# The attention output projection (Wo) as seven half-size products in two waves of eight token tiles, with the weight sums formed during attention

## The chip, the cores and the metric

The kernel runs on one core of one Trainium2 chip. The metric is device time in microseconds (us) for one execution, the median of several. The profile is one further execution, recorded by the hardware profiler.

## What is computed

An adaLN-conditioned block on 2048 tokens of width 1024. Part A is attention with a small recurrent memory (32 heads of 128, segments of 32 tokens, 8 memory rows); part B is a token-shift mixer and an MLP. Cut to what matters here:

```python
h = _layernorm(x) * (1 + ca) + sa
# A: per head q, k, v = h @ Wq, Wk, Wv; o = softmax(q k^T * scale, masked) @ v
o = jnp.einsum('bhte,hed->btd', o, Wo)      # the product that changes: [2048, 4096] @ [4096, 1024]
x = x + ga * o
h = _layernorm(x) * (1 + cb) + sb
x = x + gb * B(h, w1, w2, w3, w4)           # B starts with layernorm(h) @ w1
```

The kernel estimates the memory rows from segment means instead of running the recurrence, checks the estimate (`check_a`, `check_b` in the code), and holds a second, sequential path, which a flag selects at run time and which does not run on this input.

## The kernel before

**Attention.** A loop over 16 pairs of heads interleaves, unit by unit, the projections of the next pair (`P_units`, with `D_units` as seven half-size products in fp16, the Winograd form of Strassen's scheme) with the attention of the current heads (`scores`, `outs`). The context of a head is turned by a DMA transpose (`flip`), and `keep_o` (L755) stores it with a POOL DMA as `OTx_d`, by blocks of 512 tokens and groups of 8 heads. `guard_units` (L674, L678) loads w3 and w4 in 28 pieces into a one-buffer pool (`wstream`) and sums squares on ACT. About 1.75 heads of attention are left as a tail, which is interleaved with the first Wo units. `preload` fetches the first Wo and context tiles ahead.

**Wo.** `W_units(blk)` handles 512 tokens in four blocks. For each column half `n2` (512 columns) it runs over four groups of 8 heads (`hc`) and four token tiles (`tt`), 8 matmuls each into one PSUM bank per tile (L901), so 1024 matmuls of 128x128 by 128x512 in all. At the last group DVE multiplies the bank by the row `ga_b` into the fp32 row tile `x1` (L906). Wo is streamed in 1 MiB pieces (L884, four buffers), contexts in 1 MiB pieces (L867, six buffers); `paced` and `pace` tie the first loads to matmuls so that SP issues them in a chosen order.

**Rows.** `C1a(t)` takes a 128-token tile through: load x (L1018, SP), add (L1019, POOL), store `x_d` (ACT queue), first layernorm (`ln_act`: bn_stats on DVE L104, power on POOL L110, scale and shift on ACT L1009), modulation (L1024, L1025, DVE), store `u_d`, second layernorm. `C1b(t)` turns the tile by DMA into `zT` (L1037, ACT queue). `lagged` and `interleave` place four tiles beside the Wo units of the next block; the last four go beside `A_units(0)` and `A_units(1)`, the product with w1 (L1068) with GELU on ACT (L1069). `A_units(3)` needs the last tile. `check_b` (L984 to L999) reduces the tests to one flag; its instructions are issued early in Wo.

**What sets the order.** Each engine runs its instructions in order, and SP, ACT and POOL each issue their DMAs in order with the rest of their queue. A scheduler puts the instructions of the program into per-engine orders by dependence and place in the program; buffers of a pool are reused in turn, and a tile waits until the former user of its buffer is done. `keep_order` marks instructions whose order is fixed.

Of the kernel before, what the change touches and what calls it, by code (L numbers as in the profile page):

```python
# [9 lines left out]
BF16 = mybir.dt.bfloat16  # L10
# [13 lines left out]
H = 32  # L24
# [36 lines left out]
def kernel(ctx, tc, A_x, A_mem0, A_Wq, A_Wk, A_Wv, A_Wo, A_seg_len, B_x, B_w1, B_w2, B_w3, B_w4, c, w_mod, out,  # L61
# [14 lines left out]
    OTx_d = dram.tile([4, 4, DH, 8, 512], BF16, name="OTx_d")  # L76
    Mnew_d = dram.tile([P, KT, NSEG * M], F32, name="Mnew_d")
# [23 lines left out]
    def layernorm_stats(pool, src):  # L101
        st = pool.tile([P, 2, 6], F32, name="ln_st")
        for i in range(2):
            nc.vector.bn_stats(out=st[:, i, :], in_=src[:, i * 512:(i + 1) * 512])  # L104
        mv = pool.tile([P, 2], F32, name="ln_mv")
        nc.vector.bn_aggr(out=mv[:], in_=st[:])
        ve = pool.tile([P, 1], F32, name="ln_ve")
        nc.vector.tensor_scalar(ve[:], mv[:, 1:2], EPS, None, ALU.add)
        rstd = pool.tile([P, 1], F32, name="ln_rstd")
        nc.gpsimd.tensor_tensor(rstd[:], ve[:], mhalf[:], ALU.pow)  # L110
        return mv[:, 0:1], rstd[:]
# [55 lines left out]
    def first_pass(late_hook):  # L167
# [14 lines left out]
        wsq = mpool.tile([P, 28], F32, name="wsq")  # L182
        rin_all = mpool.tile([P, H, NT], F32, name="rin_all")
# [466 lines left out]
        pre = {}  # L650

        def preload():

            pre["ot"] = [prep.tile([P, 4, 512], BF16, name=f"pre_o{i}") for i in range(2)]
            pre["wo"] = [prep.tile([P, 4, 512], BF16, name=f"pre_w{i}") for i in range(2)]
            for i in range(2):
                nc.sync.dma_start(pre["wo"][i][:], Wo2[i * 512:(i + 1) * 512, 0:512].rearrange("(h p) n -> p h n", p=P))
                nc.sync.dma_start(pre["ot"][i][:], OTx_d[0, 0, :, 4 * i:4 * i + 4])
# [6 lines left out]
        def guard_units():  # L665

# [12 lines left out]
            nop = lambda: None  # L679
            for i in range(28):  # L680
                units += [load(i), nop, nop, square(i)]
            return units
# [69 lines left out]
        def keep_o(h):  # L752
            OT = last_ot[h] = state.pop(("ot", h))
            flat = OT[:].rearrange("p t c -> p (t c)")[:, 64:64 + S]
            nc.gpsimd.dma_start(OTx_d[:, h // 8, :, h % 8, :].rearrange("b d t -> d b t"), flat.rearrange("p (b t) -> p b t", t=512))  # L755
# [83 lines left out]
        RG = ExitStack()  # L839
        rgp = RG.enter_context(tc.tile_pool(name="x_gb", bufs=1, side="right"))  # L840
        RX = ExitStack()
        rp = RX.enter_context(tc.tile_pool(name="x_rows", bufs=1, side="right"))
        gb_b = rgp.tile([P, D], F32, name="gb_b")
# [3 lines left out]
        RW = ((ga_b, rows_d[0]), (sb_b, rows16_d[0]), (cb1_b, rows16_d[1]))  # L847
        acc_pools[:] = [psA, psA, psX, psX2]
        acc_ctr[0] = 3
        RO = ExitStack()  # L850
        wspR = RO.enter_context(tc.tile_pool(name="x1_wsR", bufs=4, side="right"))
        otcp = RO.enter_context(tc.tile_pool(name="x1_ot", bufs=1, side="right"))
        ws_pools[:] = [wspR]
        ots = {}

        paced = {}

        def pace(ld, mm):
            if mm is not None:
                tc.add_manual_dep(ld.ins, mm.ins.name, mybir.DependencyInfo(mybir.DependencyClass.Sync, mybir.DependencyReason.DATA), reason="order of loads")  # L860

        def load_ot(j, mm=None):
            if j >= 16:
                return
            ot = otcp.tile([P, 8, 512], BF16, name=f"OTc{(j + 2) % 6}")
            n = 6 if j == 3 else 8
            pace(nc.sync.dma_start(ot[:, 0:n], OTx_d[j // 4, j % 4, :, 0:n]), mm)  # L867
            ots[j] = [ot[:, 0:4], ot[:, 4:8]]

        ots[0] = [t[:] for t in pre["ot"]]  # L870

        marks = {}
# [3 lines left out]
        def W_units(blk):  # L876
            st = {}

            def load_w(n2, hc, mm=None):
                if (blk, n2, hc) == (0, 0, 0):  # L880
                    st[n2, hc] = [t[:] for t in pre["wo"]]
                elif (n2, hc) not in st:
                    woc = ws_tile([P, 8, 512])
                    pace(nc.sync.dma_start(woc[:], Wo2[hc * 1024:(hc + 1) * 1024, n2 * 512:(n2 + 1) * 512].rearrange("(h p) n -> p h n", p=P)), mm)  # L884
                    st[n2, hc] = [woc[:, 0:4], woc[:, 4:8]]

            def mk(n2, hc, tt):
                def f():
                    cs = slice(n2 * 512, (n2 + 1) * 512)
                    if (hc, tt) == (0, 0):  # L890
                        st[n2] = [acc_tile() for _ in range(4)]
                    if (n2, hc, tt) == (0, 3, 0):
                        for i in range(4):
                            x1s[blk * 4 + i] = xpools["tp4"].tile([P, D], F32, name="x1")
                    accs = st[n2]
                    if tt == 0:
                        load_w(n2, hc)
                    ot, woc = ots[blk * 4 + hc], st[n2, hc]
                    for hl in range(8):
                        h = hc * 8 + hl  # L900
                        mm = nc.tensor.matmul(accs[tt][:], lhsT=ot[hl // 4][:, hl % 4, tt * P:(tt + 1) * P], rhs=woc[hl // 4][:, hl % 4, :], start=(h == 0), stop=(h == H - 1))  # L901
                    if blk == 0 and tt == 0:
                        for f in paced.pop((n2, hc), ()):
                            f(mm)
                    if hc == 3:
                        marks[blk] = nc.vector.tensor_tensor(x1s[blk * 4 + tt][:, cs], accs[tt][:], ga_b[:, cs], ALU.mult)  # L906
                    if n2 == 1 and tt == 3:
                        load_ot(blk * 4 + hc + 6)
                return f
            return [[[mk(n2, hc, tt) for tt in range(4)] for hc in range(4)] for n2 in range(2)], load_w  # L910

        W0, W0_load = W_units(0)
        W0_load(0, 1)
        load_ot(1)
        paced[0, 0] = [lambda mm: W0_load(0, 2, mm), lambda mm: load_ot(2, mm)]
        paced[0, 1] = [lambda mm: W0_load(1, 0, mm)]
        paced[0, 2] = [lambda mm: W0_load(1, 1, mm), lambda mm: [pace(nc.gpsimd.dma_start(t[:], src.partition_broadcast(P)), mm) for t, src in RW]]
        paced[1, 0] = [lambda mm: W0_load(1, 2, mm), lambda mm: load_ot(3, mm)]
        paced[1, 1] = [lambda mm: W0_load(0, 3, mm)]
        paced[1, 2] = [lambda mm: W0_load(1, 3, mm), lambda mm: load_ot(4, mm)]  # L920
        paced[0, 3] = [lambda mm: load_ot(5, mm)]
        load_wo2(NHP - 2)
        interleave(att[done:], M_units(NHP - 3) + [lambda: load_wo2(NHP - 1)] + W0[0][0] + W0[0][1])
        for u in W0[0][2]:
            u()
# [3 lines left out]
        for u in M_units(NHP - 2):  # L929
            u()  # L930
# [3 lines left out]

# [1147 lines left out]
```

## Time and profile before

| what | value |
|---|---|
| median of 3 runs | 1466.67 us (1463.84 to 1469.35) |
| the profiled execution's own time | 1465.43 us |
| its span | 1463.6 us |
| mean granted TensorE clock | 0.994 |
| tail of attention and hand-over to Wo | 757 to 797 us |
| Wo after that | 797 to 993 us |
| product with w1 | 993 to 1048 us |
| MLP and the rest | 1048 to 1464 us |

In a group line of the profile the fields are: line, engine, operation, tiles written and read, shapes, count; then the busy time of the group in us and the mean duration of one in ns; then the idle time of the engine just before them and what ended most of it. Matmuls are pipelined, so durations overlap. In a line by stretches (windows) each stretch has its length, the busy time and count of PE, weight loads, DVE, ACT and POOL, the granted clock, the DMA share and GB/s. In the timeline, a line has start, duration, engine, line and operation, with idle time before it in brackets.

### The profile page before, as it was taken

To read this page: it belongs to the slowest core of one execution; us is meant where nothing else is said; L and a number is where in the kernel's file an instruction comes from. 1 tells how busy PE (TensorE), PEld (TensorE's weight loads), DVE (VectorE), ACT (ScalarE), POOL (GpSimd) and SP (SyncE) were. 2 spreads that over 40 slices of the span, in tenths; PEclk is the share of its full clock that TensorE was granted. 3 is DMA by queue.
4 is the path that set the end of the run, shared out by engine and by line. 5 is a ranking of instruction groups with operands and counts; after the bars stand their busy time and mean duration, and the time that the engine had idled before them with its cause. 6 is when DMAs were issued, how large, how long until landed. Compare 5 with 4: busy or idle time off the path is not lost.

```text
span 1463.6 us, 24731 instructions
## 1 busy us (share of the span) xinstructions
PE 1421.2 (97%) x9254; PEld 752.2 (51%) x9254; DVE 897.9 (61%) x1945; ACT 683.3 (47%) x1439; POOL 347.5 (24%) x494
## 2 busy tenths in 40 slices
PE   6999999999999999999998999999998999999998
PEld 4665555565555555555563444444443444444443
DVE  6627767677777777676651436335254578666684
ACT  3636666666566566566650122114466650056400
POOL 6020010000000000000001323203023664645625
PEclk9999999999999999999999999999998999999999
DMA  9778777796777787667599999965499774477812
GB/s 336 279 225 195 170 165 168 172 214 140 179 167 168 176 195 176 161 154 168 118 240 311 365 311 368 320 167 164 141 282 239 232 255 141 150 227 253 282 41 79
DMA packets 404149, 303.48 MB, mean 207 GB/s; under 512 B 199082, under 2 KB 356778, under 8 KB 402226
## 3 DMA queue, kind: packets, MB, share of 16 engines
q1 hardware_dynamic: 365904, 242.06, 62.0%
q10 hardware_dynamic: 29330, 30.89, 6.9%
q0 software_dynamic: 8784, 28.85, 6.3%
q8 instruction: 74, 1.21, 0.4%
q14 instruction: 57, 0.47, 0.1%
HBM read 200.56 MB, written 50.63 MB: 172 GB/s over the span
## 4 chain that ended last, share of the span: by engine, by line
PE 80%; DMA 10%; issue 3%; DVE 3%; ACT 3%; POOL 1%; SPq 0%; ACTq 0%; DVEq 0%; POOLq 0%
PE acc L619 31%; PE acc L901 7%; PE bank_b L1291 7%; PE bank_b L1240 6%; PE acc L1068 4%; PE acc L328 4%; PE bank_d L1240 3%; PE acc L318 3%; PE bank_d L1291 2%; PE bank_e L1291 2%; PE ps_o L730 2%; PE ps_s L713 2%; PE acc L1168 2%; PE bank_e L1240 1%; DMA xt<-in_A_x_dram 1%
## 5 line engine op out<-in xcount | busy, mean ns | idle before, releaser
L901 PE MATMUL acc<-wstream,OTc 128*128 128x512 bf16 x960 | 209.2, 379 | 4.2 <-DMA OTc<-OTx_d 3.6
L619 PEld LDWEIGHTS <-T 128*128 128x128 f16 x1408 | 130.8, 97 | 120.3 <-issue 1.4
L587 ACT COPY snap<-acc 128x480 f32<-128x480 f32 x264 | 146.7, 564 | 87.5 <-PE acc L619 82.5
L619 PE MATMUL acc<-hh,T 128*128 128x480 bf16 (+1 forms) x704 | 161.9, 366 | 0.3 <-DVE VT L591 0.3
L619 PE MATMUL acc<-hs,T 128*128 128x480 f16 x704 | 157.0, 366 | 0.4 <-ACT snap L587 0.4
L901 PEld LDWEIGHTS <-OTc 128*128 128x128 bf16 x960 | 93.3, 98 | 116.0 <-DMA OTc<-OTx_d 4.3
L1240 PEld LDWEIGHTS <-ring 128*128 128x128 f16 (+1 forms) x784 | 77.3, 99 | 106.4 <-issue 16.3
L755 POOL DMA_DIRECT2D OTx_d<-OT x32 | 24.8, 776 | 445.1 <-DMA OT<-O 366.6
L717 ACT ACTIVATE E<-ps_s 99x495 bf16<-99x495 f32 (+2 forms) x160 | 87.5, 547 | 52.4 <-PE ps_s L713 52.3
L619 PE MATMUL acc<-hh,wq 128*128 128x480 bf16 x464 | 105.1, 366 | 0.0
L737 DVE TENSOR_TENSOR O<-ps_o,rin_all 99x384 bf16<-99x384 f32 (+1 forms) x192 | 97.4, 510 | 3.9
L1205 ACT COPY snap<-bank_b 128x512 f32<-128x512 f32 x72 | 41.9, 587 | 105.3 <-PE bank_b L1291 60.6
L1291 PEld LDWEIGHTS <-hq 128*128 128x128 bf16 (+1 forms) x560 | 54.8, 98 | 66.1 <-DVE hq L1094 0.2
L591 DVE TENSOR_TENSOR KT<-acc,snap 128x480 bf16<-128x480 f32 x116 | 75.1, 655 | 19.8 <-PE acc L619 13.6
L719 DVE TENSOR_TENSOR E<-E,maskB 99x495 bf16<-99x495 bf16 (+1 forms) x128 | 48.2, 377 | 60.8 <-ACT E L717 59.5
L1094 DVE TENSOR_TENSOR ring<-ring 128x1024 f16<-128x1024 bf16 (+1 forms) x64 | 81.2, 1287 | 4.9 <-PE bank_b L1291 4.4
L730 PE MATMUL ps_o<-V,E 99*128 99x129 bf16 (+1 forms) x704 | 80.4, 220 | 3.2 <-DVE E L719 1.6
L1009 ACT ACTIVATE u<-x,ln_nmr,ln_rstd 128x1024 bf16<-128x1024 f32 x16 | 19.7, 1231 | 128.1 <-DMA x_d<-x 76.8
L730 PEld LDWEIGHTS <-E 99*128 99x128 bf16 (+1 forms) x704 | 56.8, 98 | 39.0 <-DVE E L719 3.1
L1244 ACT ACTIVATE hq<-join 128x512 bf16<-128x512 f32 x84 | 52.9, 630 | 43.6 <-DVE join L1248 43.6
L1291 PE MATMUL bank_b<-ring,hq 128*128 128x512 f16 (+1 forms) x336 | 73.2, 379 | 0.0
L591 DVE TENSOR_TENSOR VT<-acc,snap 128x480 bf16<-128x480 f32 x90 | 58.0, 651 | 18.7 <-PE acc L619 14.6
(240 smaller groups left out, 2502.8 us busy)
## 6 DMA issues: line engine op xcount, KB each, us to landing
wstream<-in_A_Wo_dram SPq DMA_DIRECT2D x31, 1024.0 KB, 10.1
OTx_d<-OT POOLq DMA_DIRECT2D x32, 512.0 KB, 7.2
wstream<-in_B_w_dram SPq DMA_DIRECT2D x28, 512.0 KB, 5.8
OTc<-OTx_d SPq DMA_DIRECT2D x14, 1024.0 KB, 7.9
ring<-in_B_w_dram SPq DMA_DIRECT2D x28, 512.0 KB, 6.2
ring<-in_B_w_dram SPq DMA_DIRECT2D x8, 1792.0 KB, 10.9
wq<-in_A_Wq_dram SPq DMA_DIRECT2D x16, 512.0 KB, 4.5
wk<-in_A_Wk_dram SPq DMA_DIRECT2D x16, 512.0 KB, 5.6
```

The costliest lines, as they stand in the source:

```text
L328: nc.tensor.matmul(acc[:, 0:CONV], lhsT=W[:, kt, hl * P:(hl + 1) * P], rhs=hh[:, kt, MAIN:MAIN + CONV], start=(kt == 0), stop=(kt == KT - 1))
L587: nc.scalar.copy(t[:], st[q][bank][:, 0:CH])
L591: nc.vector.tensor_tensor(view(d, i), chunks(st[q][bank]), chunks(st[q][s_]), ALU.add)
L619: nc.tensor.matmul(acc[:, 0:CH], lhsT=B[:, k, :], rhs=A[:, k, :], start=(j in (1, 2, 5) and k == 0), stop=(k == 3), skip_group_check=True)
L717: nc.scalar.activation(E[:rows, 0:o], ps[:rows, 0:o], ACT.Exp, scale=DH ** -0.5)
L730: nc.tensor.matmul(ps[:, i, :], lhsT=state["e", h, t // 5][:k, c:c + P], rhs=V[:k, t, 0:DH + 1], start=True, stop=True)
L737: nc.vector.tensor_tensor(O[:rows, ts[0]:ts[0] + n, :], ps[:rows, 0:n, 0:DH], rin[:, :, None].to_broadcast([rows, n, DH]), ALU.mult)
L901: mm = nc.tensor.matmul(accs[tt][:], lhsT=ot[hl // 4][:, hl % 4, tt * P:(tt + 1) * P], rhs=woc[hl // 4][:, hl % 4, :], start=(h == 0), sto ...
L1068: nc.tensor.matmul(acc[:], lhsT=w1s[:, kt, ct * P:(ct + 1) * P], rhs=zT[:, kt, b * 512:(b + 1) * 512], start=(kt == 0), stop=(kt == KT - 1))
L1094: return nc.vector.tensor_tensor(dst, a, b, op)
L1240: nc.tensor.matmul(acc[:], lhsT=B[:, k, q * P:(q + 1) * P], rhs=A[:, k, :], start=(start and k == 0), stop=(k == 3), skip_group_check=True)
L1291: nc.tensor.matmul(acc[:], lhsT=L3[:, k, i * P:(i + 1) * P], rhs=R3[:, k, :], start=(start and k == 0), stop=(k == 13), skip_group_check=True)
```

## The change

Wo becomes seven products of half size in both tokens, heads and columns (again the Winograd form). Tokens are taken in two waves of 1024; in a wave the halves are two blocks of 512 tokens. Heads are split into even and odd, columns into two halves of 512. So `A11, A12, A21, A22` are contexts of block 0 even, block 0 odd, block 1 even, block 1 odd heads, and `B11 ... B22` quarters of Wo. Each product has K = 2048 (two halves `hf` of 8 head pairs), four token tiles and 512 columns: 64 matmuls. The order is 1, 2, 5, 3, 6, 7, 4; products 1, 2 and 4 use A unchanged, the others fp16 sums, which DVE forms in place (`X_sum`, `sums`, 8 instructions of 128x4096 in a wave).

The weight sums are formed once, in attention: `guard_units` gets 16 more loads of Wo (512 KB), each followed by four DVE subtractions and a POOL store into `WoT_d`. Contexts are stored as `OTw_d`, by parity of the head. Five SBUF slots of 16 KB per partition hold contexts and sums, and later w1, w2, zT's second half and h1T. `tp` has 2 buffers instead of 3. `check_b` comes after `A_units(0)` and `A_units(1)`, and also tests the variances of all 16 tiles (`ves`). `gb_b` is loaded later, `sb_b` and `cb1_b` by `rows2`. Tiles 0 to 3 are chained beside products 7 and 4 of wave 0, tiles 4 to 7 beside products 1, 2, 5 of wave 1, tiles 8 to 11 beside 7 and 4 of wave 1, tiles 12 to 15 beside `A_units(0)` and `A_units(1)`.

```diff
-            nc.gpsimd.dma_start(OTx_d[:, h // 8, :, h % 8, :].rearrange("b d t -> d b t"), ...)
+            nc.gpsimd.dma_start(OTw_d[h % 2][:, :, h // 2, :].rearrange("b d t -> d b t"), ...)
...
+            def wo_load(k):
+                def f():
+                    st["w", k] = ws_tile([P, 2, 2, 512])
+                    keep_order(nc.sync.dma_start(st["w", k][:], Wo2[k * 256:(k + 1) * 256, :].rearrange("(b p) (n c) -> p b n c", p=P, n=2)))
+                return f
+            def wo_sums(k):
+                def f():
+                    t = st["w", k]
+                    B11, B12, B21, B22 = (t[:, b, n, :] for b in range(2) for n in range(2))
+                    keep_order(nc.vector.tensor_tensor(f16(B11), B12, B11, ALU.subtract))
+                    nc.vector.tensor_tensor(f16(B12), B22, B12, ALU.subtract)
+                    nc.vector.tensor_tensor(f16(B22), B22, f16(B11), ALU.subtract)
+                    nc.vector.tensor_tensor(f16(B21), B21, f16(B22), ALU.subtract)
+                    nc.gpsimd.dma_start(WoT_d[:, :, k, :].rearrange("j p c -> p j c"), t[:].rearrange("p b n c -> p (b n) c"))
+                return f
             for i in range(28):
                 units += [load(i), nop, nop, square(i)]
+                if i % 7 in (0, 2, 4, 6):
+                    k = i // 7 * 4 + i % 7 // 2
+                    units += [wo_load(k), nop, nop, wo_sums(k)]
...
+        SLOTS = [{(0, 0): "s0", (0, 1): "s4", (1, 0): "s2", (1, 1): "s1", "X": "s3"},
+                 {(0, 0): "s3", (0, 1): "s4", (1, 0): "s0", (1, 1): "s2", "X": "s1"}]
+        RAW = {1: (0, 0), 2: (1, 0), 3: (1, 1)}
+        SUM = {5: 0, 7: 1, 4: 2, 6: 3}
+        ORDER = (1, 2, 5, 3, 6, 7, 4)
...
+            def fin(t, n, acc, s=None):
+                cs = slice(n * 512, (n + 1) * 512)
+                if s is not None:
+                    nc.vector.tensor_tensor(s[:], acc[:], s[:], ALU.add)
+                nc.vector.tensor_tensor(x1s[t][:, cs], (acc if s is None else s)[:], ga_b[:, cs], ALU.mult)
+            def after(j, i):
+                x, t1, t2 = st[i], 8 * w + i, 8 * w + 4 + i
+                if j == 1:
+                    x["s1"] = snap("stA", x["b"])
+                elif j == 2:
+                    x1_new(t1)
+                    fin(t1, 0, x["d"], x["s1"])
+                elif j == 5:
+                    x["s5"] = snap("stA", x["d"])
+                elif j == 6:
+                    fin(t1, 1, x["d"], snap("st2", x["b"]))
+                elif j == 7:
+                    x1_new(t2)
+                    fin(t2, 1, x["b"], x["s5"])
+                elif j == 4:
+                    fin(t2, 0, x["b"])
+            def unit(j, hf, i):
+                def f():
+                    if i == 0:
+                        b_upto(seq.index((w, j, hf)) + 3)
+                    if hf == 0 and j == 1:
+                        st[i]["b"] = acc_tile()
+                    elif hf == 0 and j in (2, 5):
+                        st[i]["d"] = psB.tile([P, 512], F32, name="acc")
...
+                    for k in range(8):
+                        nc.tensor.matmul(acc[:], lhsT=A[:, k, i * P:(i + 1) * P], rhs=B[:, k, :], start=(j in (1, 2, 5) and hf == 0 and k == 0), stop=(hf == 1 and k == 7), skip_group_check=True)
+                    if hf:
+                        after(j, i)
+                return f
+            def X_sum(hf):
...
+                    nc.vector.tensor_tensor(f16(open_a(w, "X")[:, ks]), Av[w, (1, 0)][:, ks], Av[w, (1, 1)][:, ks], ALU.add)
+            def sums(hf):
...
+                    nc.vector.tensor_tensor(f16(A21), A11, A21, ALU.subtract)
+                    nc.vector.tensor_tensor(f16(A11), f16(X), A11, ALU.subtract)
+                    nc.vector.tensor_tensor(f16(A12), A12, f16(A11), ALU.subtract)
...
-        interleave(att[done:], M_units(NHP - 3) + [lambda: load_wo2(NHP - 1)] + W0[0][0] + W0[0][1])
+        interleave(att[done:], M_units(NHP - 3) + [lambda: load_wo2(NHP - 1)] + U0[1][0:4])
...
+            okx = ck.tile([P, NTT], F32, name="okx")
+            nc.vector.tensor_scalar(okx[:], ves[:], RMAX, None, ALU.is_le)
+            nc.vector.tensor_reduce(oks[:], okx[:], AX.X, ALU.min)
+            nc.vector.tensor_tensor(okm[:], okm[:], oks[:], ALU.mult)
...
+        for u in U0[2][0:4] + [lambda: load_a(0, (0, 0), 0)] + U0[2][4:] + [rows2] + M_units(NHP - 1) + U0[5]:
+            u()
+        interleave(checks, U0[3] + [next_a((0, 0))] + U0[6][0:4] + [next_a((0, 1))] + U0[6][4:])
+        interleave(chain(0), U0[7][0:4] + [next_a((1, 0))] + U0[7][4:] + U0[4][0:4] + [next_a((1, 1))] + U0[4][4:])
...
+        interleave(chain(4), U1[1] + U1[2] + U1[5])
+        for u in U1[3] + [load_w1] + U1[6] + [late_slots]:
+            u()
+        interleave(chain(8), U1[7] + U1[4])
...
+        interleave(chain(12), A_units(0) + A_units(1))
+        check_b()
         for u in A_units(2) + A_units(3):
             u()
```

## The prediction

> **What bounds the kernel now.** I read the page's busy times first, then its chain of work that ended last, then the groups.
>
> ```profile
> span 1463.6 us, 24731 instructions
> ...
> PE 1421.2 (97%) x9254; PEld 752.2 (51%) x9254; DVE 897.9 (61%) x1945; ACT 683.3 (47%) x1439; POOL 347.5 (24%) x494
> ...
> PE 80%; DMA 10%; issue 3%; DVE 3%; ACT 3%; POOL 1%; SPq 0%; ACTq 0%; DVEq 0%; POOLq 0%
> ...
> L901 PE MATMUL acc<-wstream,OTc 128*128 128x512 bf16 x960 | 209.2, 379 | 4.2 <-DMA OTc<-OTx_d 3.6
> ```
>
> TensorE is the bound. The Wo product is L901: 960 matmuls here and 64 more on the preloaded tiles, 1024 in all. The 379 ns is the length of one pipelined matmul, not its price: in steady state 177 of them took 38.37 us (timeline from 954.78), 214 to 217 ns each. I use 214 (the windows of 20 us hold 93 to 94). Next, the busy times by stretch: attention's tail, the hand-over, the rest of Wo, and product w1.
>
> ```profile
> 757.00:778.20 21.20, 19.89 (x179) 11.37 (x176) 10.84 (x36) 8.56 (x21) 2.21 (x6) 1.00 1.05 316
> 778.20:797.00 18.80, 13.83 (x64) 6.15 (x65) 3.29 (x10) 0.00 (x0) 2.61 (x7) 1.00 1.03 293
> 797.00:993.20 196.20, 195.66 (x941) 89.03 (x940) 80.93 (x186) 32.21 (x40) 46.70 (x54) 1.00 0.96 301
> 993.20:1048.40 55.20, 55.20 (x257) 25.05 (x256) 19.50 (x48) 27.76 (x40) 9.93 (x13) 1.00 0.41 128
> ```
>
> The first pair is length and PE busy; the last two columns are DMA share and GB/s. PE stands still for 1.3 + 5.0 + 0.5 = 6.8 us around Wo, nearly all of it waiting for loads. DMA is full (share about 1) at 293 to 316 GB/s from 757 on. DVE has room: 81 of 196 us. In attention (400 to 600 us) PE is busy 199.58 of 200 us, so every stall put there counts.
>
> The last view is the timeline of the row chain (layernorm, modulation, layernorm, per 128-token tile) beside Wo. I looked for whether in-order DVE is on time.
>
> ```profile
> 942.74 2.12 POOL L1019 TENSOR_TENSOR x<-x,xt 128x1024 f32<-128x1024 f32 x1 [0.93 <-issue]
> 943.32 2.10 DVE L1024 TENSOR_TENSOR u<-u,cb_b 128x1024 bf16<-128x1024 bf16 x1 [0.71 <-ACT u L1009]
> ...
> 952.10 0.69 DVE L1024 TENSOR_TENSOR u<-u,cb_b 128x1024 bf16<-128x1024 bf16 x1 [1.49 <-ACT u L1009]
> ...
> 959.47 0.69 DVE L1024 TENSOR_TENSOR u<-u,cb_b 128x1024 bf16<-128x1024 bf16 x1 [1.49 <-ACT u L1009]
> ...
> 969.50 0.67 DVE L906 TENSOR_TENSOR x<-acc,ga_b 128x512 f32<-128x512 f32 x1
> ```
>
> A tile takes 7.4 us (952.10 to 959.47). The bank that L906 empties at 969.50 was full at about 960.6: Wo ends at 993.0, the second column half takes 128 x 0.214 = 27.4 us, and this bank was 5.1 us ahead of the other three. So DVE is already 9 us late, at no cost, since eight banks serve in turn.
>
> **What the Trainium skill says.** "SBUF — State Buffer", section "SBUF: two separate sides": a DVE operation with two SBUF inputs and a GpSimd operation that reads SBUF exclude each other for the whole instruction. The trace agrees: L1024 takes 2.10 us under POOL's addition and 0.69 without. "VectorE: DVE Perf Modes", "The perf-mode tier table": a 16-bit tensor_tensor has a 2x mode, 1224 ns for 2048 elements; the trace has 1222 ns for that shape and 4052 for 7168. For the new 4096-element sums I take 2.4 us between the two rows. "DMA: Bandwidth & Descriptors", "Issuing engines are not separate DMA queues": SP, ACT and POOL transfers share the 16 DMA engines; the full DMA share above agrees.
>
> **The change part by part.** Base: the profiled execution, 1465.4 us; its median over the three runs is 1466.7, 1.2 above, which I add at the end. Orders below are those of the built instructions; L930 to L1108 in this part and the next are lines of the changed kernel where they name L936, L970, L1082 or L1108.
>
> *Fewer matmuls.* 7 products x 64 x 2 waves = 896 instead of 1024: 128 x 0.214 = -27.4 us. fp16 weights load as fast (97 ns, L619). The old stand-stills go, -6.8, and all idle time is now counted anew.
>
> *Attention.* Sixteen times: a load of 512 KB, four subtractions of 512 elements (0.42 us each, L562 to L565, so 27 us of DVE in 630 that is 72% busy), and a 512 KB store from POOL (0.78 us of POOL). T_units already makes 44 such bursts and PE is not idle for them: free. But `wstream` has one buffer, so SP's next load waits for the store, SP's weight loads and transposes queue behind it, and ACT's square waits for the load, with exp and snaps behind that. Turnaround: 0.8 + 7.2 (landing of OTx_d) + 0.3 + 5.8 (landing of wstream) = 14.1 us. The order puts 3 to 5 score groups between the last subtraction and the next square, a group 4.4 us (44.2 us per head pair): 17.6 us mostly, 13.2 twice. I take +2 us; bounds 0 and 24 (15 turnarounds x 1.6 us).
>
> *Tail.* Only 32 Wo matmuls are left to fill attention's latencies instead of 64. The tail shortens by 6.9 us of work; I let 2 us be idle (0 to 4).
>
> *Wave 0, products 1, 2, 5.* The loads up to the first half of A22 (Wo halves, head tiles, wo2) are 10.1 MiB on SP, and 1 MiB of row vectors now goes ahead on POOL: 11.1 MiB = 11.7 MB at 305 GB/s = 38 us from 757, landed about 797; X adds 2.4. PE would come at 757 + 16.3 + 6.9 + 0.9 + 13.7 = 794.8: +4. Then DVE has X's second half, two Macc additions and five sums of 2.4 ahead of the first A12 sum, 16 us against 13.7 of product 5: +2. I take +6 (2 to 12). Later loads of wave 0 (about 20 MiB in 62 us up to wave 1's second half product, 340 GB/s) are tight, and hidden by the 4-deep ring in my reckoning; uncovered they cost up to 8.
>
> *Wave 1, product 2 to 5.* Product 5 reuses the four psB banks of product 2, so it waits for DVE's first addition there. DVE's order puts ahead of it, from product 6 of wave 0 on: 21 evacuations x 0.68 = 14.3; six tiles' first half (1.9 each) 11.2; five tiles' second half (3.2 each) 16.2; seven sums x 2.4 = 16.8. That is 58.5 us in the 59.8 us that PE needs there (280 matmuls), before any gap. The chain of four tiles lasted 39 us before (933.5 to 972.6) for some 23 us of DVE work; half of those gaps get filled, and POOL's additions lock DVE. Left: 10 us of gaps. I take +9 (4 to 13), and +1.5 (0 to 3) for product 3, whose last bank waits for an ACT snap behind two row steps.
>
> *End of Wo.* `check_b` moves behind A_units(0, 1) and gets the variances of all tiles. PE's order has its L1082 matmul before A_units(2), 256/2 x 0.214 = 27.4 us after Wo's end E. Before, the last tile's variance was done at 1021.0, E + 28. Now its chain starts late: tiles 8 to 11 begin 30.4 us before E and need 33.4 (933.5 to 966.9) plus about 5.5 for 16 extra evacuations, so tile 12's L1108 comes one period later at E + 16 instead of E + 7.7 (1000.67). Late by 8.3: E + 28 + 8.3 + 0.9 - 27.4 = +10 us of PE idle (1.5 with no delay, 14 with POOL's lock). It also covers the late transposes for A_units(3).
>
> *At nothing:* gb_b's load (POOL idles there for 27 us; uncovered, its 7.5 us landing would delay only the later addends); w1 and w2 in freed slots (free some 50 us ahead; 15 us each if not); the snaps on ACT (0.59 us each, ACT is 16% busy in Wo; one that stands behind a row step costs its length, as counted for product 3); two `xt2` buffers for three: SP waits longer for POOL's addition, and Wo loads are queued behind it. It waited 43.5 us for that before with PE busy, under the ring of four half products (27 us of work); if that is used up, 2 us per addition.
>
> Sum: -27.4 - 6.8 + 2 + 2 + 6 + 9 + 1.5 + 10 = -3.7. 1465.4 - 3.7 = 1461.7; plus 1.2: **1463**.
>
> **Rivals.** *DVE keeps up.* If its gaps fill and ordering costs little, wave 1 loses 1, the end 3, wave 0 3, tail 1, attention 1: -34.2 + 9 = -25, 1441.6. For: DVE is only 41% busy in Wo now. Against: the 9 us lateness above.
>
> *Slower: the one-buffer turnaround in attention.* If stores and loads land slower than their medians (DMA share is already 0.72 to 0.79 there), ACT stands at each square. At 1.6 us per turnaround on PE it is 24 instead of 2: 1485. It decides from about 0.9 us per turnaround (1463 - 2 + 13.5 = 1474.5). For: ACT is 62% busy there and PE has no slack. Against: ACT's snaps have three units of cover, some 3 us.
>
> *The forecast* is that most of the gain turns into waits for DVE.
>
> **How the numbers follow.** Forecast 0.48, DVE keeps up 0.22, turnaround 0.30. The forecast's own range is 1452 to 1475. What can be told from no change is 0.5%, 7.3 us: below 1459.3 or above 1474. Faster: 0.22 + 0.13 of the forecast = 0.35. Slower: 0.27 + 0.04 = 0.31. Same: 0.34. Range 1444 to 1486: it leaves out half of the keep-up case and the end of the turnaround.
>
> **What would show it.** L970 with 896 matmuls; PE idle up to 10 us at wave 1's product 5 released by DVE's L936; PE idle about 10 us at L1082; wsq squares on ACT released by DMA if the slower rival holds. I am wrong if PE is idle under 10 us in all from wave 0 to A_units(2), or over 5 us in attention.

## The result, and the profile after

The changed kernel takes 1500.7 us (median of 4, 1499.7 to 1501.5) against 1468.0 us for the kernel before in the same series (1463.8 to 1469.8): a ratio of 1.0226, with a 95% interval from 1.0202 to 1.0251. It is slower by some 33 us, and above the predicted range.

The page of the changed kernel, its span, busy times and the Wo product:

```profile
span 1499.7 us, 24698 instructions
...
PE 1408.1 (94%) x9126; PEld 743.0 (50%) x9126; DVE 975.5 (65%) x2053; ACT 695.2 (46%) x1463; POOL 374.3 (25%) x512
...
L970 PE MATMUL acc<-wstream,s 128*128 128x512 f16 (+1 forms) x864 | 195.1, 387 | 32.2 <-ACT snap L930 11.3
```

With 32 more on the preloaded tile, L970 has the 896 matmuls foreseen. But it now has 32.2 us of idle time in front of it, where L901 before had 4.2. PE's busy time falls by 13.1 us only (1421.2 to 1408.1), although 128 matmuls of 0.214 us are gone: some matmuls have become longer, as shown below.

Next the busy times by stretch of the changed kernel (columns as in the prediction: length, busy time of PE, PEld, DVE, ACT and POOL, TensorE's clock, DMA share, GB/s):

```profile
100.00:757.00 657.00, 637.00 (x4654) 372.93 (x4653) 472.95 (x1243) 395.73 (x953) 69.77 (x157) 0.99 0.80 190
...
800.00:840.00 40.00, 27.93 (x141) 12.76 (x140) 28.15 (x29) 3.04 (x12) 14.01 (x11) 0.97 0.96 366
840.00:880.00 40.00, 37.33 (x161) 16.37 (x161) 8.68 (x14) 6.56 (x13) 8.71 (x10) 0.90 0.59 212
880.00:920.00 40.00, 31.92 (x139) 13.80 (x138) 34.23 (x53) 7.66 (x7) 15.62 (x11) 0.96 1.07 386
920.00:1019.60 99.60, 90.19 (x407) 40.05 (x406) 65.44 (x125) 24.33 (x27) 25.47 (x24) 0.98 0.64 200
1019.60:1086.10 66.50, 57.54 (x267) 25.80 (x266) 27.48 (x68) 31.27 (x43) 13.84 (x15) 0.95 0.64 170
1086.10:1499.70 413.60, 397.51 (x1825) 178.62 (x1822) 262.21 (x326) 164.69 (x269) 191.95 (x192) 0.99 0.64 196
```

and one stretch of the kernel before, for the attention:

```profile
100.00:757.00 657.00, 651.47 (x4820) 384.45 (x4818) 464.74 (x1208) 408.79 (x984) 55.39 (x149) 1.00 0.75 171
```

From 100 to 757 us PE is busy 14.5 us less than before. The first Wo matmul comes at 779.9 instead of 759.0: 20.9 us are lost before Wo has begun. From it to the last Wo matmul the changed kernel takes 239.5 us, where the kernel before took 234.0, in spite of the 34 us that were taken out. A_units take 66.5 us instead of 55.2, and what follows is 1.6 us shorter (413.6 against 415.2). 20.9 + 5.5 + 11.3 - 1.6 = 36.1 us, the growth of the span.

Who kept PE waiting from 757 to 1090 us in the changed kernel (total us, times, longest):

```profile
PE acc L970 <- ACT snap L930: 11.3, 2, 8.8
PE acc L970 <- DVE snap L936: 10.8, 8, 2.4
PE acc L1082 <- DVE bad L1080: 8.9, 1, 8.9
PE acc L970 <- DVE x L937: 4.2, 1, 4.2
PE acc L970 <- DVE Macc L721: 3.7, 2, 3.0
PE acc L970 <- DVE ves L110: 2.2, 1, 2.2
```

The longest Wo stall is one that the prediction had at nothing: product 3 of wave 0 waits for ACT. The timeline of the changed kernel there:

```profile
835.25 2.24 POOL L1043 TENSOR_TENSOR df<-Macc,Mold 128x70 f32<-128x70 f32 x1
837.52 0.26 ACT L1044 ACTIVATE df<-df 128x70 f32<-128x70 f32 x1 [2.05 <-POOL df L1043]
...
842.05 2.03 ACT L930 COPY snap<-acc 128x512 f32<-128x512 f32 x4
842.67 7.63 PE L970 MATMUL acc<-wstream,s 128*128 128x512 bf16 x22 [8.82 <-ACT snap L930]
842.68 0.11 PEld L970 LDWEIGHTS <-s 128*128 128x128 f16 x1 [7.54 <-issue]
843.06 0.15 PEld L970 LDWEIGHTS <-s 128*128 128x128 f16 x1 [0.28 <-issue]
843.48 0.15 PEld L970 LDWEIGHTS <-s 128*128 128x128 f16 x1 [0.28 <-issue]
```

Product 3 adds onto product 5 in the same bank, so it needs ACT's copy of product 5 first. In ACT's order the eight `check_a` steps stand ahead of those four copies. Each step alternates between ACT and POOL, and while DVE forms the 4096-element sums a POOL subtraction of 70 elements takes 2.24 us; later, with DVE done, the same line takes 0.30. So a stretch of 16 small ACT operations lasted from 823 to 842 us.

The last two lines show a second cost. After the stall the weight loads are 0.42 us apart, not 0.21. The clock (the third number from the end) for one stretch in attention, and for three here:

```profile
205.00:210.00 5.00, 4.72 (x22) 2.23 (x23) 2.83 (x9) 2.00 (x6) 0.00 (x0) 0.66 0.32 105
```

```profile
835.00:840.00 5.00, 0.00 (x0) 0.10 (x1) 2.32 (x1) 1.57 (x6) 3.70 (x6) 0.80 0.93 364
840.00:845.00 5.00, 2.33 (x6) 0.84 (x6) 0.00 (x0) 2.98 (x8) 1.61 (x5) 0.50 0.60 247
845.00:850.00 5.00, 5.00 (x17) 1.91 (x16) 0.00 (x0) 0.00 (x0) 0.00 (x0) 0.68 0.00 0
```

TensorE's clock is recorded at half during or just after some of the stalls. The trace has six such stretches between 100 and 1090 us, from 148.5, 206.5, 838.0, 909.7, 964.3 and 1053.0 on; the kernel before has none in that part. PE's work inside them ran at half clock for 3.4, 3.4, 5.6, 3.4, 3.4 and 3.0 us, and half of each is lost: 11.1 us in all, of which 3.4 lie in attention, 6.2 in Wo and 1.5 in A_units. "TensorE: Matmul & The Clock Gate" of the Trainium skill, section "Part 1: The HAM clock gate (the "warmup" mystery)", says that the array falls to half clock after an idle window of about 3.4 us and needs a busy one to come back. The trace agrees in kind, with steps of 3.41 us, but the stall of 2.03 us at 205 was enough: the measurement decides.

### The profile page after: what moved, and what is told of

The parts are those of the page before. It is cut to its first block, busy times and chain, and to the rows that moved or that the text cites. A ratio compares the mean times of both kernels' runs of the same rounds, so it can differ in the third digit from the quotient of the medians.

```text
span 1499.7 us, 24698 instructions
## 1 busy us (share of the span) xinstructions
PE 1408.1 (94%) x9126; PEld 743.0 (50%) x9126; DVE 975.5 (65%) x2053; ACT 695.2 (46%) x1463; POOL 374.3 (25%) x512
## 5 line engine op out<-in xcount | busy, mean ns | idle before, releaser
L970 PE MATMUL acc<-wstream,s 128*128 128x512 f16 (+1 forms) x864 | 195.1, 387 | 32.2 <-ACT snap L930 11.3
L622 PE MATMUL acc<-hs,T 128*128 128x480 f16 x704 | 160.9, 368 | 3.0 <-ACT snap L590 2.8
L970 PEld LDWEIGHTS <-s 128*128 128x128 f16 (+1 forms) x864 | 85.8, 99 | 140.6 <-issue 40.7
L779 POOL DMA_DIRECT2D OTw_d<-OT x32 | 24.8, 775 | 420.1 <-DMA OT<-O 359.2
L761 DVE TENSOR_TENSOR O<-ps_o,rin_all 99x384 bf16<-99x384 f32 (+1 forms) x192 | 97.5, 510 | 3.9
L1325 ACT COPY snap<-bank_b 128x512 f32<-128x512 f32 x72 | 41.8, 586 | 105.3 <-PE bank_b L1411 58.2
L594 DVE TENSOR_TENSOR KT<-acc,snap 128x480 bf16<-128x480 f32 x116 | 74.7, 653 | 19.4 <-PE acc L622 14.1
L759 ACT ACTIVATE O<-ps_o,rin_all 99x128 bf16<-99x128 f32 x192 | 56.5, 367 | 37.8 <-DVE rin_all L756 37.2
L594 DVE TENSOR_TENSOR VT<-acc,snap 128x480 bf16<-128x480 f32 x90 | 57.9, 652 | 20.8 <-PE acc L622 15.6
```

The lines of the kernel that those rows point to most:

```text
L594: nc.vector.tensor_tensor(view(d, i), chunks(st[q][bank]), chunks(st[q][s_]), ALU.add)
L622: nc.tensor.matmul(acc[:, 0:CH], lhsT=B[:, k, :], rhs=A[:, k, :], start=(j in (1, 2, 5) and k == 0), stop=(k == 3), skip_group_check=True)
L759: nc.scalar.mul(O[:rows, t, :], ps[:rows, i, 0:DH], rin[:, i:i + 1])
L761: nc.vector.tensor_tensor(O[:rows, ts[0]:ts[0] + n, :], ps[:rows, 0:n, 0:DH], rin[:, :, None].to_broadcast([rows, n, DH]), ALU.mult)
L970: nc.tensor.matmul(acc[:], lhsT=A[:, k, i * P:(i + 1) * P], rhs=B[:, k, :], start=(j in (1, 2, 5) and hf == 0 and k == 0), stop=(hf == 1 a ...
```

## The experiments

The theory that the profile suggests: the attention loses 21 us because SP waits for the store of the sums before it can load into the one `wstream` buffer (in the changed kernel SP stood 81.5 us in 14 waits for that store, and ACT waited 11.5 us in 4 waits for squares' loads). The Wo stalls are ACT's order, then DVE's row steps; A_units stall on `bad`. Rivals are named with each run. Lateness below is the start of a head's first exponential on ACT against the same in the kernel before, at the last head. Line numbers of the later kernels are shifted against the changed kernel's (L971 is its L970, L937 and L938 its L936 and L937). Differences in the text are of medians; those of the ratios, which compare within one series, agree with them within 3 us, but for att_alone (26 and 31 us; one of its four runs was 14 us longer than the rest).

| run | us | against before (95%) |
|---|---|---|
| after | 1500.7 | 1.0226 (1.0202 to 1.0251) |
| att_alone | 1494.0 | 1.0212 (1.015 to 1.0275) |
| ws2 | 1502.4 | 1.0223 (1.0176 to 1.027) |
| snap_first | 1491.3 | 1.0175 (1.0132 to 1.0217) |
| flag_late | 1497.4 | 1.021 (1.0172 to 1.0249) |
| nops_only | 1477.8 | 1.0068 (1.0046 to 1.0091) |
| in_nops | 1484.0 | 1.0108 (1.0085 to 1.0131) |
| no_xt | 1474.9 | 1.0058 (1.0037 to 1.008) |
| combo | 1468.1 | 1.0012 (1.0003 to 1.0021) |
| no_add | 1448.3 | 0.9882 (0.9855 to 0.9909) |
| dve_add | 1466.0 | 0.9995 (0.998 to 1.001) |
| no_sums | 1464.4 | 1.0006 (0.9987 to 1.0024) |
| xt3 | 1470.1 | 1.0031 (1.0015 to 1.0047) |
| pipe | 1465.8 | 0.999 (0.9975 to 1.0004) |
| pipek | 1467.1 | 1.0013 (1.0 to 1.0026) |
| pipe_dve2 | 1461.1 | 0.9961 (0.9948 to 0.9975) |
| pipe_dve | 1451.8 | 0.9895 (0.9871 to 0.9919) |

### Attention: the work, the buffer, or the places

**att_alone** puts the attention part alone into the kernel before.

```diff
             for i in range(28):
                 units += [load(i), nop, nop, square(i)]
+                if i % 7 in (0, 2, 4, 6):
+                    k = i // 7 * 4 + i % 7 // 2
+                    units += [wo_load(k), nop, nop, wo_sums(k)]
```

> The kernel before, with only the attention part of the change added: the sixteen loads of Wo blocks, their four subtractions and the stores. Nothing reads the sums; the Wo product itself is as before. Theory (the one-buffer turnaround stands in front of the SP queue and PE stalls 15 to 20 us in attention, some of it at half clock): 1484 to 1490 us, first Wo matmul some 18 to 21 us later than at 759.0. Rival (the 21 us come from the new layout of the head tiles or from something else in the changed kernel): 1468 to 1473 us.

1494.0 us, above the range expected: the attention part alone costs 26, and attention's last heads run 28.6 us late. The loss can be made by this part alone, without the layout of the head tiles. Why it is 8 us more than in the changed kernel (20.8) is open.

**ws2** gives the stream two buffers.

```diff
-        wsp = LX.enter_context(tc.tile_pool(name="x_ws", bufs=1))
+        wsp = LX.enter_context(tc.tile_pool(name="x_ws", bufs=2))
```

> The changed kernel with two wstream buffers in attention instead of one, so that the next load no longer waits for the store of the sums. Theory (turnaround): attention gets back 15 to 20 of its 21 us, the rest of the kernel moves along with it: 1480 to 1486 us. Rival (the load is that of the DMA traffic or of the 64 subtractions on DVE, which stay): 1497 to 1501 us.

1502.4 us. SP's waits for the store, from 100 to 760 us, first in the changed kernel, then in ws2:

```profile
SPq L678 <- DMA WoT_d<-wstream: 81.5, 14, 11.0
```

```profile
SPq L678 <- DMA WoT_d<-wstream: 9.0, 2, 5.5
```

The median time from the issue of a square's load to the square rises from 7.7 to 14.1 us, and yet the last heads run 22.0 us late, as in the changed kernel (20.8). The theory falls: the turnaround is there, but taking most of it away gives PE nothing back.

**nops_only** adds nothing at all to the kernel before but empty units, at the places of the Wo blocks.

```diff
                 units += [load(i), nop, nop, square(i)]
+                if i % 7 in (0, 2, 4, 6):
+                    units += [nop] * 4
```

> The kernel before with four empty units in its list of guard units at each of the sixteen places where the change puts a Wo block: no instruction is added, only the places of the 28 squares, of their loads and of the units around them move against the projections. Theory (the 21 us of attention come from where the squares and loads now stand, beside the short halo evacuations, and not from the sums): 1480 to 1495 us, with lags growing at the same heads (2 to 8 and 18 to 23). Rival (the added loads, subtractions and stores cost it): 1466 to 1470 us.

1477.8 us, between the two expectations: 11.7 us more for no work, and the heads run 12.3 us late at the end. (The recorded execution took 1484.2 us, the longest of four; some 6 us of it were lost behind attention, where PE waited 4.15 us for a Wo load at 921 and then ran at half clock.)

```profile
100.00:757.00 657.00, 642.55 (x4739) 378.30 (x4738) 460.14 (x1194) 400.30 (x968) 55.93 (x144) 1.00 0.74 167
```

PE is busy 8.9 us less than the 651.47 of the kernel before. **in_nops** is the opposite: all the work, with a one-buffer pool of its own (not shown), and nothing moved.

```diff
             for i in range(28):
                 units += [load(i), nop, nop, square(i)]
+            for k in range(16):
+                i = 7 * k // 4
+                units[4 * i + 2], units[4 * i + 5] = wo_load(k), wo_sums(k)
```

> The changed kernel with the Wo loads and sums put in the place of empty units that the list of guard units already had, with a buffer of their own, so that nothing else moves. The added work is all there. Theory (places): attention is back to within 3 us of before, 1480 to 1484 us. Rival (the added work): 1497 to 1503 us.

1484.0 us, 16.7 less than the changed kernel. From 100 to 757 us PE is busy 651.63 of 657 us, as before the change (651.47), and the last heads run 1.1 us late:

```profile
100.00:757.00 657.00, 651.63 (x4813) 384.45 (x4812) 484.32 (x1273) 407.77 (x978) 68.40 (x164) 1.00 0.81 196
```

DVE does 19.6 us more than before in that stretch and DMA's share is up from 0.75 to 0.81, and PE doesn't notice. The nine kernels below that have the same attention (combo to pipe_dve in the table) run 0.2 to 4.2 us late. in_nops changes the buffer too, but ws2 has shown that a second buffer at the moved places gains nothing. So the added work is nearly free, as predicted; its place in the list is not. The list of guard units is merged into the head pairs by index. With 64 more units in it the distance between a load and its user, three units, is a shorter time, and the squares, row sums and weight sums land at other points of the pair. In the changed kernel a square at 202 us lands between two small halo copies, and DVE stands for a weight load:

```profile
202.16 1.92 ACT L682 ACTIVATE wstream<-wstream 128x2048 bf16<-128x2048 bf16 x1
...
203.44 0.43 DVE L565 TENSOR_TENSOR T<-wk,wq 128x512 f16<-128x512 bf16 x1 [1.94 <-DMA wk<-in_A_Wk_dram]
...
204.07 0.44 ACT L124 CAST KT<-acc 128x136 bf16<-128x136 f32 x2
...
205.28 0.34 PE L754 MATMUL ps_o<-V,E 99*128 99x129 bf16 x3 [2.03 <-DVE O L761]
```

The copy of the second halo waits for the end of the square, and DVE, which stood 1.94 us for `wk`, is late with the evacuation (L761) that PE needs. From 100 to 757 us DVE and ACT stand for DMA (weights, row vectors, squares' loads) for 5.2 us in the kernel before, 5.4 in in_nops, 19.0 in nops_only, 25.1 in ws2, 29.6 in the changed kernel and 35.8 in att_alone. That follows the lateness (0, 1.1, 12.3, 22.0, 20.8, 28.6) with one step out of order. How much of it is the squares' places and how much the waits for loads was not separated.

### Two single stalls

**snap_first** pins the squares of `check_a` on ACT behind what is written ahead of them.

```diff
-                nc.scalar.activation(df[:], df[:], ACT.Square)
+                keep_order(nc.scalar.activation(df[:], df[:], ACT.Square))
```

(and the second square likewise)

> The changed kernel with the squares of check_a pinned on ACT behind the four snaps of product 5 of wave 0. Theory (the 8.8 us stall at product 3 is the order on ACT): the stall shrinks to the 1 us that the sum of A12 (835.0) leaves, and the half-clock time after it (2.7 us) goes too: 10 us faster, 1490 to 1492 us. Rival (DVE is the next one late, so that products 7 and 4 of wave 0 wait longer in place of it): under 4 us faster, 1497 to 1500 us.

1491.3 us, 9.4 less than the changed kernel: the stall of 8.8 is gone, 0.7 is left on the sum, and little of it came back elsewhere.

**flag_late** writes `check_b` behind all of A_units.

```diff
         interleave(chain(12), A_units(0) + A_units(1))
-        check_b()
         for u in A_units(2) + A_units(3):
             u()
+        check_b()
```

> The changed kernel with check_b behind all of A_units, so that no matmul between A_units(1) and A_units(2) needs the variance of the last tile. Theory (the 8.9 us at L1082 cover the transposes of the last tiles in part): the stall goes, and A_units(3) waits some 4 to 5 us for the last transpose, issued at 1063.0: 5 to 7 us faster, 1494 to 1496 us. Rival (the transposes are in time): 9 to 11 us faster, 1490 to 1492 us.

1497.4 us, 3.3 less. PE's waits there in flag_late:

```profile
PE acc L1182 <- ACT s L1183: 3.1, 2, 2.2
PE acc L1182 <- DMA s<-z: 2.8, 1, 2.8
```

The 8.9 us for `bad` are replaced by 5.9 of others, for ACT's evacuations and for the transposes of the last tiles: the flag was only the first of several that were late.

**combo** is in_nops, snap_first and flag_late together.

> in_nops together with snap_first and flag_late. If the three add up: 1500.7 - 18 - 9.4 - 4 = 1469 us, 1466 to 1472, level with the kernel before. If the places don't matter: 1485 to 1489 us.

1468.1 us: they add up, and the kernel is level with the one before (0.1% above). With the attention repaired and 128 matmuls fewer there is still no gain: PE stands some 26 us between 757 and 1090 us, 20 of them from product 7 of wave 0 on.

### What holds DVE up from product 7 on

In the changed kernel PE is kept by DVE evacuations (L936, L937) at products 7 and 4 of both waves and at the start of wave 1. The timeline before wave 1:

```profile
903.76 2.13 POOL L1103 TENSOR_TENSOR x<-x,xt 128x1024 f32<-128x1024 f32 x1
...
905.86 0.54 POOL L112 TENSOR_TENSOR ln_rstd<-ves,mhalf 128x1 f32<-128x1 f32 x1
...
906.38 2.11 POOL L1103 TENSOR_TENSOR x<-x,xt 128x1024 f32<-128x1024 f32 x1
...
906.44 2.07 DVE L1092 SCALAR_TENSOR_TENSOR ln_nmr<-ln_mv,ln_rstd 128x1 f32<-128x1 f32 x1 [1.63 <-POOL ln_rstd L112]
908.43 1.27 DVE L937 TENSOR_TENSOR x<-acc,ga_b 128x512 f32<-128x512 f32 x2
...
909.16 7.03 PE L970 MATMUL acc<-wstream,s 128*128 128x512 bf16 x24 [4.23 <-DVE x L937]
```

POOL's addition for one tile stands ahead of the 1/sqrt for another; DVE waits for that, then its one-element operation takes 2.07 us instead of 0.16 under the next addition, and the evacuation that PE needs stands behind both.

**no_xt** leaves out the loads and the additions of the residual input (L1102 and L1103 of the changed kernel).

```diff
-                xt = tp.tile([P, D], BF16, name="xt2")
-                for rows, toks in p_rows(t):
-                    nc.sync.dma_start(xt[rows, :], x2[toks, :])
-                nc.gpsimd.tensor_tensor(x1[:], x1[:], xt[:], ALU.add)
```

> The changed kernel without the loads of the residual input and POOL's additions of it (part of the computation is left out: the output lacks the residual input). Theory (from product 7 of wave 0 on DVE is late with its own row steps): the stalls before L970 after 880 us stay within 5 us of their 17, and the L1082 stall shortens by 2 or 3: 1493 to 1498 us. Rival (the loads, and POOL's additions with their lock on DVE, hold DVE up): 10 us or more go, 1486 to 1490 us.

1474.9 us, 25.8 less: the rival is right, and the gain is larger than it said. **no_add**, on combo, leaves out the additions alone.

```diff
-                nc.gpsimd.tensor_tensor(x1[:], x1[:], xt[:], ALU.add)
```

> combo without POOL's additions of the residual input; the loads stay (part of the computation is left out: the output lacks the residual input). Theory (POOL's additions hold DVE up: they lock it out of two-input operations and stand ahead of the 1/sqrt that DVE waits for): of combo's 20 us of stalls from product 7 of wave 0 to the last transposes 12 to 15 go, 1452 to 1456 us. Rival (the loads of the residual input come late behind the Wo loads on SP): 1464 to 1468 us.

1448.3 us, 19.8 less than combo, and below the range expected. It is the additions, not the traffic of the loads, which stay. (Nothing waits for them any more, but in combo POOL's additions had waited for them only once, 2.8 us, from 840 to 1050 us.) The PE waits, first of combo, then of no_add (757 to 1050 us):

```profile
PE acc L971 <- DVE snap L937: 10.2, 8, 2.4
PE acc L971 <- DVE x L938: 4.2, 1, 4.2
```

```profile
PE acc L971 <- DVE snap L937: 4.0, 3, 1.4
PE acc L971 <- DVE x L938: 1.8, 1, 1.8
```

**no_sums**, on combo, leaves out twelve DVE sums instead.

```diff
-                    nc.vector.tensor_tensor(f16(A21), A11, A21, ALU.subtract)
-                    nc.vector.tensor_tensor(f16(A11), f16(X), A11, ALU.subtract)
-                    nc.vector.tensor_tensor(f16(A12), A12, f16(A11), ALU.subtract)
```

> combo without the three sums of head tiles for products 3, 6 and 7 (twelve instructions of 2.3 us on DVE, 28 us; part of the computation is left out, the products run on the unsummed tiles). Theory (the stalls from product 7 on come from the row steps, not from these): 1462 to 1467 us. Rival (the sum of DVE's work counts): 1452 to 1458 us.

1464.4 us: 28 us of DVE work fewer bring 4 (by the ratios 1), and PE's waits for `snap` on DVE even rise, from 10.2 to 15.7 us. The sum of DVE's work, on which the prediction's step for wave 1 was built, is not what counts. Six runs then ask what the additions do.

**dve_add** moves them to DVE.

```diff
-                nc.gpsimd.tensor_tensor(x1[:], x1[:], xt[:], ALU.add)
+                nc.vector.tensor_tensor(x1[:], x1[:], xt[:], ALU.add)
```

> combo with the additions of the residual input on DVE instead of POOL. Theory (lock and POOL's order): the 1/sqrt is at once, the lock is gone, but DVE has 16 x 1.3 us = 21 us more to do: 1460 to 1465 us. Rival (the sum of DVE's work is what counts): 1469 to 1476 us.

1466.0 us, 2 less than combo. From the first Wo matmul on a loaded slot to the last it takes 208.2 us instead of 216.3, but A_units lose it again: PE waits 7.6 us there (the view names no releaser; the wait ends 3.2 us after the last tile's transpose was issued), and DVE, in its order, now waits for the loads of the residual input (840 to 1040 us):

```profile
DVE u L1109 <- ACT u L1094: 16.8, 12, 3.6
DVE ln_nmr L1093 <- POOL ln_rstd L112: 14.5, 25, 1.1
DVE x L1104 <- DMA xt<-in_A_x_dram: 10.7, 5, 4.1
```

**xt3** gives those loads a third buffer, with POOL adding. (To make room, a scratch tile of the tests becomes 16 bit, here and in pipe_dve; the three DVE operations on it take 2.3 us with either.)

```diff
+        txp = LT.enter_context(tc.tile_pool(name="x1_x", bufs=3))
...
-                xt = tp.tile([P, D], BF16, name="xt2")
+                xt = txp.tile([P, D], BF16, name="xt2")
```

> combo with three buffers for the loads of the residual input instead of two (one scratch tile of the check made 16 bit to find the room). Theory (the additions themselves are the trouble): 1466 to 1469 us. Rival (SP waits for the buffer, with Wo loads queued behind it, or the addition waits for its load): 1460 to 1464 us.

1470.1 us: no gain. **pipe** cuts the row step in two, so that a tile's first layernorm is written ahead of the second of the tile before; **pipek** pins one operation besides.

```diff
-            return lagged(C1a, C1b, list(range(t0, t0 + 4)), lag=1)
+            out = []
+            for i in range(t0, t0 + 6):
+                fs = [fn(i - d) for fn, d in ((C1b, 2), (C1a, 0), (C1m, 1)) if t0 <= i - d < t0 + 4]
+                out.append(lambda fs=fs: [f() for f in fs])
+            return out
```

(`C1a` now ends with the first layernorm, `C1m` holds the rest of the step)

> combo with the row step cut in two, so that the first layernorm of a tile is written ahead of the second of the tile before; the work is the same, POOL still adds. Theory (the serial order of the row steps holds DVE up): 1456 to 1463 us, and under 7 us per tile at the end. Rival (the lock, or the sum of the work): 1466 to 1471 us.

> pipe with the first multiplication of the second half pinned on DVE behind what is written ahead of it. Theory (serial order): as pipe or a little better, 1454 to 1463 us. Rival (lock or sum of work): 1466 to 1471 us.

1465.8 and 1467.1 us: the order alone brings 2 and 1, short of the range expected, and not clear of the spread of the runs. **pipe_dve** has the order, the additions on DVE and the third buffer; **pipe_dve2** the first two without the buffer.

> pipe with the additions of the residual input on DVE and three buffers for their loads. Theory (serial order and lock both count, DVE has room once its order is right): 1450 to 1458 us. Rival (sum of DVE's work): 1464 to 1472 us.

> pipe_dve with two buffers for the loads of the residual input. If the loads are in time as with POOL's additions: within 2 us of pipe_dve. If DVE now waits for them in its order (10.7 us in dve_add): 3 to 8 us slower than pipe_dve.

1451.8 and 1461.1 us. Order and place of the additions together bring 7 us, the buffer on top of them 9.3, though alone it brought nothing. What DVE waited for (840 to 1040 us), first in pipe_dve, then in pipe_dve2:

```profile
DVE ln_nmr L1094 <- POOL ln_rstd L112: 9.9, 20, 1.0
DVE u L1117 <- ACT u L1095: 3.0, 1, 3.0
```

```profile
DVE ln_nmr L1093 <- POOL ln_rstd L112: 10.1, 20, 1.0
DVE x L1106 <- DMA xt<-in_A_x_dram: 6.3, 2, 5.1
```

Against dve_add the waits for ACT fall from 16.8 us to 3.0 and those for the residual input from 10.7 to none that the list shows. From the last Wo matmul to the last tile's second layernorm it takes 29.6 us instead of 41.8 in combo, and PE has no stall left in A_units. pipe_dve is the best whole kernel of the study, 1.05% faster than before (0.81 to 1.29%) and 3.3% faster than the change as it was made.

## Why the prediction was wrong, step by step

| step | predicted | came |
|---|---|---|
| fewer matmuls, old stand-stills | -27.4 - 6.8 | the same |
| attention | +2 (0 to 24) | +20.9 |
| tail | +2 (0 to 4) | +0.5 |
| wave 0, products 1, 2, 5 | +6 (2 to 12) | +5.9 |
| wave 0, product 3 (snaps on ACT) | nothing | +8.8, +2.8 at half clock |
| wave 0, products 7 and 4, start of wave 1 | nothing | +8.1, +1.7 |
| wave 1, product 2 to 5 | +9 (4 to 13) | +2.6 |
| wave 1, product 3 | +1.5 (0 to 3) | +2.5, +1.7 |
| wave 1, products 7 and 4 | nothing | +4.1 |
| end of Wo, `check_b` | +10 (1.5 to 14) | +8.9, +1.5 |

With the -1.6 of the part after A_units the third column adds up to 34; the 2 us that are missing to the span's growth of 36 are gaps too small to list.

**The failed step is attention's +2.** The prediction wrote "T_units already makes 44 such bursts and PE is not idle for them: free", and about the work it was right: in_nops does all of it and is late by 1.1 us. But it counted only what is added and not what the addition moves. nops_only shows 12 us for positions alone. The other 9 appear only when the work stands at the moved places; how they come about is not shown, and in att_alone it is 16 (28.6 against 12.3). The prediction's own sign of being wrong, PE idle over 5 us in attention, came: from 100 to 757 us it is busy 637.0 us, 14.5 less than before. With 2 instead of 20.9 the kernel would stand at about 1482, inside the range.

That is half of the miss. The other half, some 20 us, lies in Wo and A_units: the stalls that were put at nothing came to 21.0 us (8.8, 8.1 and 4.1) and half clock to 7.7, while wave 1's products 2 to 5 came 6.4 below their price.

**The slower rival had nearly the price and the wrong mechanism.** It gave 24 us to the one-buffer turnaround. The turnaround happened (median 7.7 us from load to square, and 18.7 before), but ws2 takes most of it away without a gain. Its sign came too, squares on ACT released by DMA (11.5 us in 4 waits): a sign can come without its mechanism.

**"The snaps on ACT" at nothing** failed by the same kind of omission: the prediction asked whether ACT has time (16% busy), not what stands ahead of the copies in its order. That was `check_a`, which goes in lockstep with POOL; DVE's sums lock POOL, and so eight steps lasted 19 us. snap_first gives 9.4 back.

**Wave 1's +9** had the engine right and the place and the reason wrong. From product 7 of wave 0 on the stalls for DVE sum to 15.0 us (10.8 + 4.2 + 2.2, less the 2.2 at product 5 of wave 0), but the largest part comes at products 7, 4 and 1, while the rows of the wave are being worked. The prediction counted DVE's work (58.5 us in 59.8); no_sums and no_add show that 28 us of that work bring 4 at most and the additions on POOL, no DVE work at all, 20. "POOL's additions lock DVE" was in the text as a side remark, without a term in the sum; the quoted pair of lines, 2.10 and 0.69 us, was the price that was left out.

**The end** was right in place and size (10 against 8.9 and 1.5).

**Wave 0, products 1, 2 and 5** came out at 5.9 against 6, in part by luck. The load-bound X is there: it began at 815.8, after DVE had stood 1.7 us for the first half of A22, and PE's 2.2 us for `snap`, which is behind X on DVE, follow from it. But the longest wait of the three is another, which had no term:

```profile
801.75 0.53 DVE L1064 TENSOR_SCALAR low<-rin_all 128x704 f32<-128x704 f32 x1 [11.70 <-DMA OTw_d<-OT]
...
805.01 0.81 DVE L721 TENSOR_TENSOR Macc<-acc,Macc 128x284 f32<-128x284 f32 x2
805.51 10.52 PE L970 MATMUL acc<-wstream,s 128*128 128x512 bf16 x48 [2.99 <-DVE Macc L721]
```

By the profile DVE stood 11.7 us for the store of a context, with the reductions of the tests (L1064 to L1074) next in its order, and PE waited for the addition behind them.

One reading of the lines was too wide: DMA is full only up to 993 us; the fourth line by stretch has a share of 0.41 after that. The sum doesn't rest on it.

**No term for the clock.** Each long stall cost up to 2.8 us more than its length, 11 us in all.

Open is the split of attention's loss between squares and loads, the part of it that the work at the moved places makes, and how far the gain of pipe_dve is the lock and how far POOL's order: taking POOL out removes both.

## What to carry to other kernels

Where background units are merged into a stream by index, adding a unit moves all others: compare where the old ones land, not only what the new ones cost, and put new work into empty places. For an in-order engine ask what stands ahead of the operation that the bound engine needs, and whom that waits for; the busy share doesn't tell. When several serial causes lie behind one stall, removing each alone may show next to nothing (dve_add 2, pipe 2, xt3 less than nothing) and all three together 16 us (pipe_dve).

## What the runs showed of the hardware that was not expected

A stall of 2.0 us was enough to bring half clock for 3.41 us (at 205), while one of 3.0 us (802.5 to 805.5) was not followed by any; matmuls of 512 columns are then 0.427 us apart instead of 0.214. What tells them apart can be worked out from the trace. The changes of the clock record lie on one grid of steps of 3.413 us: from 148.5 to 206.5 are 17 steps, from there to 838.0 another 185. In the step just ahead of each of the six falls PE was idle for 2.03 to 3.41 us; in none of the other steps at full clock from 100 to 1100 us for more than 1.88. The stall of 3.0 us was split by the grid into 1.3 and 1.7. All 18 traces of this case agree: 2.03 us or more ahead of 66 falls, at most 2.05 in 5116 other steps. So in these runs the price of a stall depended on where it fell in the grid, and not only on its length.

The lock between DVE and POOL catches the smallest operations: a POOL subtraction of 70 elements took 2.24 us beside DVE's sums and 0.30 alone, and a DVE operation on one element per partition 2.07 instead of 0.16 us beside POOL's addition. "SBUF — State Buffer" of the Trainium skill, section "SBUF: two separate sides", has this in both directions: the one that starts first holds the other off for its whole instruction. The trace bears it out: the DVE operation began at 906.44, 0.06 us into the POOL addition, and ended with it, at 908.5.
